# Bias rows for all 576 columns in place of rows for distances, in an attention and MLP kernel on one core

## The chip, the cores and the metric

The kernel runs on one core of a Trainium2 chip. The time is the device time of one execution in microseconds. Three runs of the kernel before gave 711.92, 712.65 and 712.97 us; their median is 712.65 us. One more execution was recorded by the hardware profiler. On a core, TensorE (PE in the profile) multiplies matrices, VectorE (DVE), ScalarE (ACT) and GpSimd (POOL) work element by element, and SyncE (SP) issues most transfers.

## What is computed

Attention with a bias made by a small network from relative positions, for 4 batches, 8 heads, 576 positions and 64 values a head, followed by a two-layer MLP over all 2304 tokens:

```python
scores = scale * np.matmul(q, k.transpose(0, 1, 3, 2))
rel = (pos[:, None] - pos[None, :]).astype(np.float32)
psi_rel = np.log1p(np.abs(rel))
psi_i = np.log1p(np.maximum(pos[:, None].astype(np.float32), 1.0))
x = (psi_rel / psi_i)[..., None]
h = np.maximum(x @ w1 + b1, 0.0)          # 32 hidden units
bias = h @ w2                             # 8 heads
scores = scores + bias.transpose(2, 0, 1)[None, :, :, :]
attn = softmax(scores); attn_out = attn @ v
...
h = x @ w_in; g = np.maximum(h, 0.0) + alpha * np.minimum(h, 0.0)
out = g @ w_out                           # 512 -> 2048 -> 512
```

The bias does not depend on the batch. For a query i and a key j it depends on |i - j| and on i, and the reference spells the softmax with its maximum taken off.

## The kernel before

The program is written as a list of some 2,800 operations, each with its choices of engine. Nothing is ordered at run time: a table `ISSUE` holds the order of all operations and the engine chosen for each (`58` is operation 58 by its first choice, `66.1` by its second), a table `SLOT` the buffer of every value, and a table `IDLE` the places where TensorE gets matmuls that compute nothing, to keep it busy (`796:2` puts two of them ahead of operation 796; they are issued by L994). Each engine works through its own part of the list in order. Numbers count the operations in the order in which the program makes them.

The stages are these. `bias_tile` (L465), 36 times, makes the bias of 16 query positions for all 8 heads, 128 rows, and writes it to a scratch in DRAM. `weights` (L645), 8 times, unpacks and splits the weights of 256 hidden columns. `qk_turn` transposes queries and keys, `v_rows` prepares values. `unit` (L752), 32 times, does the attention of two heads for 256 or 320 queries: it loads bias rows from the scratch, multiplies (L601 in float32 for batch 0, L602 in float16 pairs for the others), adds the bias and takes the maximum (L796), exponentiates (L799), normalises (L809 to L820), transposes (by TensorE at L828 for batch 0, by DMA at L815 for the others) and multiplies by the values (L857 or L849). `chunk` runs the MLP on 256 tokens at a time, first layer at L927, second at L946. The first MLP chunk needs attention of all heads of batch 0 for its queries, and the weights.

A bias tile has four rows of hidden values, each for 4 query positions times 32 units on 128 partitions (L474 to L483). A row is relu(R + psi), where R holds log1p(distance) times a scale for distances 0 to 575, once for all partitions; a row is made for as many distances as the tile needs, max(576 - 16t, 16t + 16) for tile t. It can be made by ScalarE (L478), VectorE (L475) or GpSimd (L481). One product by TensorE (L487 to L496) turns the four rows into 128 rows of bias: it walks the distances downwards up to a column `l0` and upwards behind it, so that one relative column axis serves all 16 positions, 591 columns in three pieces, each with four matmuls of 32 output partitions. ScalarE (L506) or VectorE (L507) takes the result from PSUM, and one DMA (L510) writes it to the scratch with a row pitch that shifts each position by one element, so that the loads of `unit` (L769, L782) read rows of 576 in true columns.

At the start, the constants (R, psi and its inverse, the identity and a mask; 900 columns) are loaded by L419, w1 by L416, and VectorE scales R (L426) behind a maximum over w1 (L421).

Of the kernel before, what the change touches and what calls it, by code (L numbers as in the profile page):

```python
# [25 lines left out]
RW = S  # L26
SK = 15
HQ = S + 32
IQ = H * HQ - 1
# [114 lines left out]
"""  # L144
IDLE = """
30:23 62:2 118:2 90:1 104:1 111:2 683:2 55:3 97:3 132:1 641:2 676:4 959:1 662:1 139:2 634:2 697:1 160:2 669:4 718:5 725:4 704:1 711:1 739:7 388:1
569:3 549:2 767:1 563:1 353:3 596:3 611:1 800:1 419:1 614:1 806:2 814:8 828:4 796:2
"""

# [118 lines left out]
def attention_then_moe(ctx: ExitStack, tc, q, k, v, w1, b1, w2, w_in, w_out, alpha, cst, out):  # L268
# [64 lines left out]
    def rows_of(blk, at, dims):  # L333
        x = scr[blk]
        return bass.AP(x.tensor, x.offset + 16 + at, dims)


    o_ = lambda name, val: opt.get(name, val)
    col = [0]
# [706 lines left out]
```

## Time and profile before

| | |
|---|---|
| median of three runs | 712.65 us |
| profiled execution | 711.24 us |
| its span, first to last instruction | 709.5 us |
| busy: TensorE, VectorE, ScalarE, GpSimd | 673.0, 513.7, 397.4, 167.7 us |
| matmuls that compute nothing (L994) | 111 |
| bias products (L496) | 864 records, 24 a tile |

Busy time says how long an engine had an instruction at work, not whether the end of the kernel waited for it. TensorE runs at one of two clock levels, and the profile gives the granted share of the upper one. What an engine waited for, and what ended the wait, is read from the views of waits and of the chain that ended last.

### The profile page before, as it was taken

The page shows a single profiled execution, that of the slowest core. Times are in us where ns is not written, and L with a number is a line of the kernel's source. Part 1 is how long each engine was busy: PE and PEld are TensorE (multiplying, and loading weights), DVE is VectorE, ACT ScalarE, POOL GpSimd, SP SyncE. Part 2 cuts the span into 40 slices and gives each one's busy share as a digit, 9 for nine tenths or more (in the row PEclk, how much of TensorE's full clock was granted, in tenths as well). Part 3 has the DMA queues.
Part 4 walks back from the last instruction along what each step waited for, and adds up shares of the span by engine and source line. Part 5 has one row for each costly group of instructions (what it writes and reads, how often), then busy time and mean ns, then how long its engine had stood idle before and what let it go on. Part 6 is the DMA issues. An engine that isn't in the chain of part 4 may idle for free.

```text
span 709.5 us, 15371 instructions
## 1 busy us (share of the span) xinstructions
PE 673.0 (95%) x5732; PEld 422.9 (60%) x5732; DVE 513.7 (72%) x1245; ACT 397.4 (56%) x809; POOL 167.7 (24%) x223
## 2 busy tenths in 40 slices
PE   7988878879999999999999999999999999999997
PEld 2554434445765666666666666666666666666664
DVE  6799999997898789897878777677666755333222
ACT  3888989676776566564565655644454534221321
POOL 1124253223222132221213130221221221111110
PEclk8999999999999999999999999999999999999999
DMA  9899987855589889999999998999788885100000
GB/s 208 218 296 303 289 296 255 283 183 152 117 199 219 185 175 219 222 215 190 219 198 221 194 202 161 177 211 205 170 188 190 173 142 109 19 30 1 30 1 30
DMA packets 236554, 125.89 MB, mean 177 GB/s; under 512 B 204864, under 2 KB 204864, under 8 KB 236480
## 3 DMA queue, kind: packets, MB, share of 16 engines
q1 hardware_dynamic: 233888, 124.90, 75.8%
q8 instruction: 45, 0.74, 0.5%
q10 hardware_dynamic: 2592, 0.01, 0.2%
q14 instruction: 29, 0.24, 0.1%
HBM read 73.87 MB, written 15.61 MB: 126 GB/s over the span
## 4 chain that ended last, share of the span: by engine, by line
PE 71%; DVE 18%; issue 4%; DMA 3%; ACT 2%; POOL 1%; ACTq 0%; SPq 0%; DVEq 0%; POOLq 0%
PE H L927 25%; PE O L946 24%; PE S L602 6%; PE A L849 6%; DVE five L669 3%; DVE fg L796 3%; PE A L857 2%; PE S L496 2%; PE S L828 2%; PE S L576 2%; PE S L601 1%; DMA at<-a 1%; DVE wout L387 1%; DVE mg L935 1%; DVE fg L507 1%
## 5 line engine op out<-in xcount | busy, mean ns | idle before, releaser
L927 PE MATMUL H<-x,win 128*128 128x256 f16 x1728 | 200.7, 273 | 1.3 <-DVE mg L935 1.2
L946 PE MATMUL O<-wout,mg 128*128 128x512 f16 x864 | 198.7, 379 | 1.6 <-DVE st L796 0.8
L927 PEld LDWEIGHTS <-win 128*128 128x128 f16 x1728 | 166.6, 98 | 34.0 <-issue 7.1
L799 ACT ACTIVATE fg<-fg,st 128x576 f32<-128x576 f32 x144 | 110.7, 769 | 55.4 <-DVE st L796 48.0
L946 PEld LDWEIGHTS <-mg 128*128 128x128 f16 x864 | 82.0, 98 | 95.1 <-issue 6.5
L934 ACT ACTIVATE mg<-H,sm 128x256 f32<-128x256 f32 x144 | 62.3, 469 | 135.4 <-PE H L927 121.0
L935 DVE SCALAR_TENSOR_TENSOR mg<-H,sm,mg 128x256 f32<-128x256 f32 x144 | 64.8, 478 | 101.0 <-ACT mg L934 100.7
L796 DVE CUSTOM_DVE_ANT_0 fg<-S,fg 128x576 f32<-128x576 f32 x127 | 93.8, 750 | 17.3 <-PE S L602 14.9
L812 DVE SCALAR_TENSOR_TENSOR a<-fg,st,a 128x576 f16<-128x576 f32 x108 | 90.0, 834 | 21.0 <-POOL a L809 16.1
L809 POOL TENSOR_SCALAR a<-fg,st 128x576 f16<-128x576 f32 x65 | 54.1, 834 | 177.2 <-DMA at<-a 70.1
L940 POOL TENSOR_TENSOR mg<-mg 128x512 f16<-128x512 f32 x33 | 41.2, 1247 | 157.4 <-ACT mg L938 68.1
L496 PE MATMUL S<-at,w2b 128*32 128x79 f32 (+35 forms) x684 | 50.1, 345 | 8.3 <-ACT fg L506 3.4
L602 PE MATMUL S<-qk 64*128 64x288 f16 (+1 forms) x678 | 53.3, 284 | 0.7 <-DVE qk L583 0.7
L849 PE MATMUL A<-at,five 128*64 128x256 f16 (+3 forms) x720 | 51.5, 288 | 0.0
L496 PEld LDWEIGHTS S<-at,w2b 128*32 128x32 f32 x684 | 25.3, 112 | 36.7 <-issue 9.6
L602 PEld LDWEIGHTS <-qk 64*128 64x128 f16 (+1 forms) x720 | 32.7, 96 | 23.4 <-issue 17.2
L849 PEld LDWEIGHTS <-five 128*64 128x64 f16 (+1 forms) x720 | 36.0, 109 | 14.7 <-issue 11.3
L478 ACT ACTIVATE at<-cst 128x464 f32<-128x464 f32 (+17 forms) x62 | 39.1, 658 | 8.0 <-PE S L496 4.5
L810 ACT ACTIVATE a<-fg,st 128x576 f16<-128x576 f32 x43 | 32.9, 769 | 18.6 <-DMA at<-a 11.3
L481 POOL TENSOR_SCALAR at<-cst,npsi 128x416 f32<-128x416 f32 (+15 forms) x32 | 24.9, 785 | 58.0 <-PE S L496 33.2
L994 PE MATMUL H<-sm 128*128 128x512 f16 x111 | 33.5, 412 | 0.9 <-DVE w2b L405 0.9
L819 POOL TENSOR_SCALAR fg<-fg,st 128x576 f32<-128x576 f32 x29 | 23.2, 808 | 44.6 <-DVE st L804 24.6
(148 smaller groups left out, 796.2 us busy)
## 6 DMA issues: line engine op xcount, KB each, us to landing
fg<-scr SPq DMA_DIRECT2D x64, 576.0 KB, 4.9
scr<-fg SPq DMA_DIRECT2D x36, 295.5 KB, 4.5
x<-in_moe_w_in_dram SPq DMA_DIRECT2D x10, 512.0 KB, 5.4
x<-in_moe_w_out_dram SPq DMA_DIRECT2D x10, 512.0 KB, 5.4
fg<-scr SPq DMA_DIRECT2D x32, 144.0 KB, 4.9
out_dram<-mg SPq DMA_DIRECT2D x18, 256.0 KB, 2.6
five<-in_q_dram SPq DMA_DIRECT2D x32, 128.0 KB, 4.4
five<-in_k_dram SPq DMA_DIRECT2D x32, 128.0 KB, 3.8
```

The source lines that it names most:

```text
L496: nc.tensor.matmul(ps.t[32 * gl:32 * gl + 32, c:n], lhsT=w2b, rhs=x, start=True, stop=True)
L602: return [(lambda a, dst=dst, zq=zq, zk=zk, i=i: nc.tensor.matmul(dst(a), lhsT=tr16(qt)[at, 0, pr, zq, lo:lo + n], rhs=tr16(qt)[at, 1, pr, ...
L796: V(lambda x=x, sl=sl, st=st, ls=ls: nc.vector.tensor_tensor_reduce(out=in_halves(ls[x]()), in0=halves(sl[x].t), in1=in_halves(ls[x]()), s ...
L799: A(lambda x=x, st=st, ls=ls: nc.scalar.activation(ls[x](), ls[x](), AF.Exp, bias=st.t[:, x:x + 1], scale=-1.0, accum_out=st.t[:, 2 + x:3 ...
L809: pl.op([("POOL", 775, lambda x=x, rec=rec, ls=ls, a16=a16: nc.gpsimd.tensor_scalar(a16.t[:, 0:S], ls[x](), rec(), 1.0, op0=ALU.mult, op1= ...
L812: V(lambda x=x, rec=rec, ls=ls, a16=a16: nc.vector.scalar_tensor_tensor(a16.t[:, 640:640 + S], ls[x](), rec(), a16.t[:, 0:S], op0=ALU.mult ...
L849: nc.tensor.matmul(ps.t[64 * hh:64 * hh + 64, 0:w], lhsT=v5[0:hi, zv, n, 2 * pr + hh, :], rhs=at16(at)[0:hi, 5 * za + n, 320 * hh:320 * hh ...
L927: nc.tensor.matmul(hb.t[:, f, :], lhsT=win[:, fp, zw, kb, P * f:P * f + P], rhs=x[:, zx, kb, :], start=(n == 0), stop=(n == 11))
L934: A(lambda f=f: nc.scalar.activation(gf(f), hb.t[:, f, :], AF.Copy, scale=cu[:, f:f + 1]), 470, ky, [hb, t_sig], [(g, f)])
L935: V(lambda f=f: nc.vector.scalar_tensor_tensor(gf(f), hb.t[:, f, :], cs[:, f:f + 1], gf(f), op0=ALU.mult, op1=ALU.max), 475, ky, [hb, t_si ...
L940: ("POOL", 1210, lambda: nc.gpsimd.tensor_tensor(gv(1), g.t, gv(0), op=ALU.subtract))], ky, [g, (gg, 0)], [(gg, 1)], tag="g1", cont=True)
L946: nc.tensor.matmul(ob.t[:, t, :], lhsT=gg.t[:, zg, f, P * t:P * t + P], rhs=wout[:, fp, zw, f, :], start=(first and f == 0 and (zg, zw) == ...
```

## The change

R becomes a table of 1148 columns that holds the distance for a running column offset, with the partition's own position inside the group of four taken into account. A row for group g is then R from column 572 - 4g on, 576 columns, on whichever engine. The product reads the four rows in two pieces, 512 and 64 columns, forwards. The result of 576 columns goes to a scratch of plain shape (positions, heads, columns), and the loads read two neighbouring heads as one run. The tiles of `fg` lose their 16 spare columns. The tables `ISSUE`, `SLOT` and `IDLE` are new as a whole; only the head of the first and the last is shown.

```diff
-RW = S
-SK = 15
-HQ = S + 32
-IQ = H * HQ - 1
+RC = S - 4
+RW = S + RC
...
 ISSUE = """
-3 5.1 0 203 2 8.1 1 207 11.1 17 14.1 12 15.1 6.1 16.1 7.1 204 205 9.1 206 13.1 208 10.1 209 18.1 210 215 219 33 211 19 20 21 22 24 34 23 25 29 26 58
...
 IDLE = """
-30:23 62:2 118:2 90:1 104:1 111:2 683:2 55:3 97:3 132:1 641:2 676:4 959:1 662:1 139:2 634:2 697:1 160:2 669:4 718:5 725:4 704:1 711:1 739:7 388:1
-569:3 549:2 767:1 563:1 353:3 596:3 611:1 800:1 419:1 614:1 806:2 814:8 828:4 796:2
+30:30 767:1 648:3 655:2 289:3 634:3 111:2 739:2 139:2 195:2 83:2 132:2 421:1 153:4 55:4 62:5 118:2 223:1 732:3 676:6 125:4 959:2 146:3 697:2 518:3
+669:3 521:3 538:2 552:2 529:2 662:1 577:1 753:1 611:1 771:2 782:3 793:7 625:2
...
-    fg = sb.tile([P, n_f, S + 16], F32, name="fg")
+    fg = sb.tile([P, n_f, S], F32, name="fg")
...
-    scr = [dp.tile([1, (min(256, S - i) * H + 1) * HQ], F32, name=f"scr{i}") for i in range(0, S, 256)]
+    scr = [dp.tile([min(256, S - i), H, S], F32, name=f"scr{i}") for i in range(0, S, 256)]
...
-                nc.scalar.activation(hb.t[:, 0:wd], R[:, 0:wd], AF.Relu, bias=PSI[:, g:g + 1], scale=1.0)
+                nc.scalar.activation(hb.t, R[:, lo:lo + S], AF.Relu, bias=PSI[:, g:g + 1], scale=1.0)
...
-            cuts = sorted({0, l0, 512, S + SK})
-            for c, n in zip(cuts, cuts[1:]):
+            for c, n in pieces:
                 for gl in range(4):
-                    x = hs[gl].t[:, 0:wd]
-                    if n <= l0:
-                        x = bass.AP(x.tensor, x.offset + l0 - c, [list(x.ap[0]), [-1, n - c]])
-                    else:
-                        x = x[:, c - l0:n - l0]
-                    nc.tensor.matmul(ps.t[32 * gl:32 * gl + 32, c:n], lhsT=w2b, rhs=x, start=True, stop=True)
...
+                    nc.tensor.matmul(ps.t[32 * gl:32 * gl + 32, c:n], lhsT=w2b, rhs=hs[gl].t[:, c:n], start=True, stop=True)
...
-        DMA(lambda e: e.dma_start(out=rows_of(blk, row * IQ - SK, [[HQ, P], [1, S + SK]]),
-                                  in_=ev_t()[:, 0:S + SK]), P * S * 3.4, key, [ev], [(scr_tok[16 * t // P], row)])
...
+        DMA(lambda e: e.dma_start(out=scr[blk][r0:r0 + 16].rearrange("r h j -> (r h) j"), in_=ev.t), P * S * 3.4, key, [ev], [(scr_tok[16 * t // P], r0)])
...
-                last[0] = DMA(lambda e, blk=blk, r=r, L=L: e.dma_start(out=L.t, in_=rows_of(blk, P * r * IQ + hp * HQ, [[IQ, P], [HQ, 2], [1, S]])),
+                last[0] = DMA(lambda e, blk=blk, r=r, L=L: e.dma_start(out=L.t, in_=scr[blk][P * r:P * r + P, hp:hp + 2, :]),
...
-    r = np.broadcast_to(np.log1p(u.astype(np.float32))[None, :], (P, RW))
+    rel = (u[None, :] - RC - i[:, None]).astype(np.float32)
+    r = np.log1p(np.abs(rel))
```

The new issue list begins with `3 8.1 1 269 2 11.1 5 0 14.1 17 13.1 18 12.1 6.1 16.1 7.1 19 270 271`: the load of w1 is operations 5, 8, 11 and 14, the constants are 17, the maximum over w1 is 19, and 269 to 272 are the first half of a weight tile.

## Rows read from the trace of the kernel before

**Rows 1.** The page, busy us of each engine, share of the span and instructions

```profile
PE 673.0 (95%) x5732; PEld 422.9 (60%) x5732; DVE 513.7 (72%) x1245; ACT 397.4 (56%) x809; POOL 167.7 (24%) x223
```

**Rows 2.** Busy us (instructions) by stretch, granted clock, DMA share, GB/s

```profile
31.40:159.10 127.70, 106.97 (x1075) 56.50 (x1071) 123.13 (x273) 104.19 (x181) 44.85 (x59) 1.00 0.86 271
159.10:240.00 80.90, 80.43 (x632) 51.74 (x633) 67.00 (x191) 54.76 (x116) 20.45 (x32) 1.00 0.73 170
240.00:360.00 120.00, 115.11 (x980) 76.30 (x978) 100.89 (x250) 68.62 (x144) 30.47 (x40) 1.00 1.03 206
360.00:709.50 349.50, 344.08 (x2818) 225.60 (x2815) 201.38 (x478) 151.82 (x342) 66.61 (x82) 1.00 0.64 132
```

**Rows 3.** Page's group (busy, mean ns | idle), and TensorE's timeline (start us, us)

```profile
L994 PE MATMUL H<-sm 128*128 128x512 f16 x111 | 33.5, 412 | 0.9 <-DVE w2b L405 0.9
158.12 0.60 PE L994 MATMUL H<-sm 128*128 128x512 f16 x2
```

**Rows 4.** The chain that ended last (start us, us): last long VectorE entry

```profile
151.36 1.20 DVE five L669 x2
```

**Rows 5.** Timeline of TensorE at an undisturbed bias tile

```profile
24.54 1.21 PE L496 MATMUL S<-at,w2b 128*32 128x47 f32 x24
25.68 0.86 PE L576 MATMUL O<-cst,five 128*128 128x128 f32 x5
```

**Rows 6.** Groups by line: rows and evictions of the bias

```profile
L478 ACT ACTIVATE at<-cst 128x464 f32<-128x464 f32 (+17 forms) x62 | 39.1, 658 | 8.0 <-PE S L496 4.5 <-DVE cst L427 1.9 <-PE O L496 1.3
L475 DVE TENSOR_SCALAR at<-cst 128x384 f32<-128x384 f32 (+16 forms) x35 | 14.9, 453 | 5.6 <-PE S L496 5.5
L506 ACT ACTIVATE fg<-S,cst 128x591 f32<-128x591 f32 x24 | 19.8, 835 | 4.0 <-PE S L496 4.0
L507 DVE TENSOR_SCALAR fg<-S,cst 128x591 f32<-128x591 f32 x8 | 7.1, 884 | 0.0
```

**Rows 7.** Groups by line and shape on GpSimd, rows of the bias

```profile
L481 POOL TENSOR_SCALAR at<-cst,npsi 128x416 f32<-128x416 f32 x4 | 3.6, 920 | 4.1 <-PE O L496 4.1
L481 POOL TENSOR_SCALAR fg<-cst,npsi 128x560 f32<-128x560 f32 x1 | 0.7, 736 | 0.0
L481 POOL TENSOR_SCALAR at<-cst,npsi 128x576 f32<-128x576 f32 x1 | 1.1, 1117 | 0.1
```

**Rows 8.** A score product, ten transpositions, a value product; a copy by VectorE

```profile
159.77 1.19 PE L601 MATMUL S<-qk 64*64 64x288 f32 x8
...
165.32 1.24 PE S L828 x10
172.70 2.99 PE A L857 x20
...
L839 DVE COPY at<-S 128x640 f32<-128x640 f32 x3 | 2.5, 823 | 1.1 <-PE S L828 1.1
```

**Rows 9.** Transfer, SP's and VectorE's timeline, stretch and waits at the start

```profile
cst<-in_const_dram SPq DMA_DIRECT2D x1, 450.0 KB, 3.3
4.72 0.34 SPq L419 DMA_DIRECT2D cst<-in_const_dram  x1
4.73 0.43 DVE L666 TENSOR_SCALAR win<-mg 128x512 int32<-128x512 int32 x1 [2.46 <-DMA mg<-in_moe_w_in_dram]
5.20 1.42 DVE L669 SCALAR_TENSOR_TENSOR win<-mg,win 128x512 int32<-128x512 int32 x2
10.33 0.52 DVE L426 TENSOR_SCALAR cst<-cst,sm 128x576 f32<-128x576 f32 x1
10.00:20.00 10.00, 7.63 (x77) 3.38 (x81) 6.71 (x20) 6.42 (x10) 2.38 (x3) 0.66 1.01 178
DVE at L475 <- PE S L496: 5.5, 5, 2.9
```

**Rows 10.** Waits (us, times, longest), up to 165 us and behind

```profile
PEld S L496 <- POOL at L481: 4.6, 8, 1.5
POOL a L809 <- DMA at<-a: 70.1, 23, 6.6
```

More of the change, by code (lines that the diff above doesn't have):

```diff
@@ L311, in attention_then_moe @@
     n_f = 10
-    fg = sb.tile([P, n_f, S + 16], F32, name="fg")
-    c_f2 = Slots("f2", [fg[:, 2 * i:2 * i + 2, 0:S] for i in range(n_f // 2)])
-    c_f = Slots("f", [fg[:, i, 0:S] for i in reversed(range(n_f))], [{("f2", i // 2, i % 2)} for i in reversed(range(n_f))])
+    fg = sb.tile([P, n_f, S], F32, name="fg")
+    c_f2 = Slots("f2", [fg[:, 2 * i:2 * i + 2] for i in range(n_f // 2)])
+    c_f = Slots("f", [fg[:, i] for i in reversed(range(n_f))], [{("f2", i // 2, i % 2)} for i in reversed(range(n_f))])
     for i in range(n_f // 2):
@@ L330, in attention_then_moe @@
     c_st = slots("st", 10, [P, 8])
-    scr = [dp.tile([1, (min(256, S - i) * H + 1) * HQ], F32, name=f"scr{i}") for i in range(0, S, 256)]
-    def rows_of(blk, at, dims):
-        x = scr[blk]
-        return bass.AP(x.tensor, x.offset + 16 + at, dims)
+    scr = [dp.tile([min(256, S - i), H, S], F32, name=f"scr{i}") for i in range(0, S, 256)]
     o_ = lambda name, val: opt.get(name, val)
@@ L467, in bias_tile @@
         hs, made = [], []
-        r0, l0 = S - 16 * t, 16 * t + SK
-        wd = max(r0, l0 + 1)
         for gl in range(4):
@@ L472, in bias_tile, with on_dve, on_act, on_pool @@
             hb = Buf(c_h)
-            def on_dve(g=g, hb=hb):
-                nc.vector.tensor_scalar(hb.t[:, 0:wd], R[:, 0:wd], PSI[:, g:g + 1], 0.0, op0=ALU.add, op1=ALU.max)
-            def on_act(g=g, hb=hb):
-                nc.scalar.activation(hb.t[:, 0:wd], R[:, 0:wd], AF.Relu, bias=PSI[:, g:g + 1], scale=1.0)
-            def on_pool(g=g, hb=hb):
-                nc.gpsimd.tensor_scalar(hb.t[:, 0:wd], R[:, 0:wd], 3.0e38, npsi[:, g:g + 1], op0=ALU.min, op1=ALU.max)
-            made.append(pl.op([("ACT", 286 + 0.833 * wd, on_act), ("DVE", 210 + 0.521 * wd, on_dve), ("POOL", 320 + 1.03 * wd, on_pool)], key, [t_R, t_T, t_N], [hb], tag="H", cont=True))
+            lo = RC - 4 * g
+            def on_dve(g=g, hb=hb, lo=lo):
+                nc.vector.tensor_scalar(hb.t, R[:, lo:lo + S], PSI[:, g:g + 1], 0.0, op0=ALU.add, op1=ALU.max)
+            def on_act(g=g, hb=hb, lo=lo):
+                nc.scalar.activation(hb.t, R[:, lo:lo + S], AF.Relu, bias=PSI[:, g:g + 1], scale=1.0)
+            def on_pool(g=g, hb=hb, lo=lo):
+                nc.gpsimd.tensor_scalar(hb.t, R[:, lo:lo + S], 3.0e38, npsi[:, g:g + 1], op0=ALU.min, op1=ALU.max)
+            made.append(pl.op([("ACT", 766, on_act), ("DVE", 510, on_dve), ("POOL", 900, on_pool)], key, [t_R, t_T, t_N], [hb], tag="H", cont=True))
             hs.append(hb)
@@ L487, in mm @@
         def mm():
-            cuts = sorted({0, l0, 512, S + SK})
-            for c, n in zip(cuts, cuts[1:]):
+            for c, n in pieces:
                 for gl in range(4):
-                    x = hs[gl].t[:, 0:wd]
-                    if n <= l0:
-                        x = bass.AP(x.tensor, x.offset + l0 - c, [list(x.ap[0]), [-1, n - c]])
-                    else:
-                        x = x[:, c - l0:n - l0]
-                    nc.tensor.matmul(ps.t[32 * gl:32 * gl + 32, c:n], lhsT=w2b, rhs=x, start=True, stop=True)
-        PE(mm, 1260, key, hs + [t_w2], [ps])
+                    nc.tensor.matmul(ps.t[32 * gl:32 * gl + 32, c:n], lhsT=w2b, rhs=hs[gl].t[:, c:n], start=True, stop=True)
+        PE(mm, 1130, key, hs + [t_w2], [ps])
         ev = Buf(c_f)
-        ev_t = lambda: fg[:, n_f - 1 - ev.slot]
         def shift():
@@ L504, in shift, with ev_act, ev_dve @@
             return MASK[:, m:m + 1]
-        pl.op([("ACT", 935, lambda: nc.scalar.activation(ev_t()[:, 0:S + SK], ps.t[:, 0:S + SK], AF.Identity, scale=EVI[:, t:t + 1], bias=shift())),
-               ("DVE", 935, lambda: nc.vector.tensor_scalar(ev_t()[:, 0:S + SK], ps.t[:, 0:S + SK], EVI[:, t:t + 1], shift(), op0=ALU.mult, op1=ALU.add))],
-              key, [ps, t_c, t_beta], [ev], tag="ev")
-        blk, row = divmod(16 * t, 256)
-        DMA(lambda e: e.dma_start(out=rows_of(blk, row * IQ - SK, [[HQ, P], [1, S + SK]]),
-                                  in_=ev_t()[:, 0:S + SK]), P * S * 3.4, key, [ev], [(scr_tok[16 * t // P], row)])
+        def ev_act():
+            nc.scalar.activation(ev.t, ps.t[:, 0:S], AF.Identity, scale=EVI[:, t:t + 1], bias=shift())
+        def ev_dve():
+            nc.vector.tensor_scalar(ev.t, ps.t[:, 0:S], EVI[:, t:t + 1], shift(), op0=ALU.mult, op1=ALU.add)
+        pl.op([("ACT", 830, ev_act), ("DVE", 830, ev_dve)], key, [ps, t_c, t_beta], [ev], tag="ev")
+        blk, r0 = divmod(16 * t, 256)
+        DMA(lambda e: e.dma_start(out=scr[blk][r0:r0 + 16].rearrange("r h j -> (r h) j"), in_=ev.t), P * S * 3.4, key, [ev], [(scr_tok[16 * t // P], r0)])
     order = [None]
@@ L781, in unit @@
                 for hh in range(2):
-                    last[0] = DMA(lambda e, L=L, hh=hh: e.dma_start(out=L.t[64 * hh:64 * hh + 64], in_=rows_of(2, (hp + hh) * HQ, [[IQ, 64], [1, S]])),
+                    last[0] = DMA(lambda e, L=L, hh=hh: e.dma_start(out=L.t[64 * hh:64 * hh + 64], in_=scr[2][:, hp + hh, :]),
                                   64 * S * 3.4, ky, [scr_tok[4]], [(L, ("b", hh))], keep=1 - hh, after=last[0], off="kL")
```

213 rows, old and new, of tables (ISSUE, SLOT) are left out of this document.

## Prediction, made before the change was run

> **What bounds the kernel now.** I read the whole-run page first, then the busy time by stretch, then the chain of waits, then the groups by line. The page alone misleads: it has TensorE busy for 673.0 us of 709.5 and VectorE for 72% [rows 1], which looks like a kernel bound by TensorE throughout. By stretch it falls in two. From 31.4 to 159.1 us VectorE is busy 123.13 of 127.7 us and ScalarE 104.19, while TensorE has 106.97, and part of that is idle filling: the 111 matmuls of L994 compute nothing, and the last two run from 158.12 us [rows 2, 3]. From 159.1 us to the end TensorE is busy 80.43 of 80.9, 115.11 of 120 and 344.08 of 349.5 us, so it is idle for 10.8 us in 550 [rows 2]. The chain says the same: long VectorE entries up to 151 us, then almost only matmuls [rows 4]. So the time is: the moment at which TensorE has no more gap, plus the TensorE work left at that moment. Before it, an operation costs what it costs VectorE, and ScalarE behind it. After it, only TensorE work costs anything.
>
> All 36 bias tiles stand ahead of that moment, in the issue list of either kernel. That decides how each edit is priced.
>
> **The product.** An undisturbed tile at the upper clock level starts at 24.54 us and lets the next work start at 25.68: 1.14 us for 591 columns in three pieces [rows 5]. After it is 576 columns in two pieces. By columns alone that is 1.11 us, by pieces alone 0.76; I take 1.06, near the end by columns, since the pieces that go are the short ones. So it gives 1 to 14 us over 36 tiles, 3 by the value taken. None of it counts in the sum: TensorE has 20.7 us of idle and most of its fillers in that part [rows 2, 3], and its waiting there is the cover. Were the cover gone, those 3 us would be gained.
>
> **The rows.** A tile needs four rows of max(576-16t, 16t+16) distances, on average 440; after, always 576. Over 36 tiles this is 63,360 columns against 82,944. The new table also moves them: ScalarE 72 to 76 rows, VectorE 36 to 26, GpSimd 36 to 42. At 576 columns I take 0.762 us on ScalarE (0.658 at the mean, plus 130 columns at 0.83 ns), 0.505 on VectorE (0.453, plus 130 columns at some 0.4 ns), and 0.90 on GpSimd, between 0.736 for a row of 560 and 1.117 for the one row of 576 [rows 6, 7]. The evictions go from 27 on ScalarE and 9 on VectorE to 21 and 15; they cost 0.835 and 0.885 for 591 columns, so some 0.82 and 0.87 for 576 [rows 6]. Summed durations: ScalarE 69.8 to 75.1 us, VectorE 24.3 to 26.2, GpSimd 27.7 to 37.8. That is 17 us more elementwise work, 10 of it on the engine with the most room.
>
> **Where TensorE stops waiting.** The new table reorders the whole program, so the rows alone say little; the two tables can be counted. The idle string tells where each table still expects a gap. Before, the last entry is 796:2, ahead of the transposition group that starts at 159.1 us. After, it is 625:2. I counted in each issue list what stands on VectorE ahead of that point and what is left on TensorE behind it. The last layers are untouched in both: all 72 first-layer groups and 87 second-layer operations are left, and all of batches 1 to 3. The difference on TensorE: after has one two-head score product less to do (1.12 us of the 1.19 shown, since the next work starts before its end), four transposition groups (0.60 each) and one value product (2.99), by the times of these lines [rows 8]: 6.5 us less is left. On VectorE, each price 0.06 us under its duration because its next operation starts before the last has ended: rows 36 to 26, -2.6 us; evictions 9 to 15, +4.7; weight unpacking 32 short and 64 long operations to 29 and 58, -4.9 (0.43 and 0.71 each); copies out of transpositions none to 4, +3.0 (0.823 each); evictions of queries and keys none to 3, +2.1 (not seen on VectorE; by that copy of 640 columns at 0.82); score additions 24 to 26 with their small operations, +2.7; the rest -1.1. Together +3.9 us [rows 6, 8, 9]. So at this mark after stands 2.7 us better. The mark before it (814:8 and 793:7) gives another reading: VectorE 0.9 us less, TensorE 1.0 us more left, together +0.1. I take the middle, -1.3 us, with both ends kept. ScalarE ahead of the last mark has 5.7 us more (122.7 to 128.4, of 159), GpSimd 11.0 more (50.6 to 61.6): neither fills the stretch, so I put nothing for them here and the rest into a rival.
>
> **The start.** The constants grow from 900 to 1472 columns, 450 to 736 KB. Before, their transfer was issued at 4.72 us and landed 3.3 us later; at the 178 GB/s of that stretch the other 286 KB are 1.6 us, so 9.6 us, if SP issues it no sooner [rows 9]. The scaling of that table started at 10.33 us, behind 4.9 us of unpacking and a maximum, from 4.73 us on; after, only one half of a weight tile stands ahead of it, and it is 0.2 to 0.3 us longer for 1148 columns. So the rows can begin between 0.6 us earlier and at the same time as before. But VectorE has then done 4.8 us of work instead of 7.0, since the first maximum now waits for w1 ahead of all unpacking, which is queued behind it. That is +1.6 to +2.2 us that VectorE must do later. Against it: the clock was 0.66 between 10 and 20 us, the two first tiles ran at the lower level, and VectorE waited 5.5 us in all on tiles [rows 9]. The table has 30 fillers ahead of the first product, not 23, which shortens the pause in front of it by up to 1.5 us; if the clock holds, up to 3 us come back. I take +1.5, with -1 and +2.2 as ends.
>
> **The scratch.** Bias rows are written as 128 runs of 576 values, not 591, and pairs of heads are read in one run of 4608 bytes, not two of 2304. What they feed is bound by VectorE in the first part and by TensorE in the second; I put it at nothing, with up to 3 us of gain (second rival).
>
> **Sum.** -1.3 + 1.5 = +0.2 us on the profiled execution of 711.24 us (span 709.5). That execution lies 1.4 us under the median of the runs, 712.65; the difference is carried over, so 712.9 us.
>
> **Rival one, slower: rows made on GpSimd come late.** Rows on GpSimd differ far more than the columns explain: the four of 416 columns took 0.920 us on average, one of 560 took 0.736 [rows 7]. TensorE waited for such rows eight times, 4.6 us [rows 10]. After has 42 of them, all at full width. If they take 1.1 us instead of 0.9, GpSimd has 8.4 us more, in tiles that the attention units of batch 0 need; half to all of it then reaches VectorE as waiting. That gives 717 to 721 us. It decides if the mean row on GpSimd passes 1.0 us and VectorE is idle for over 9 us between 31 and 159, where it is now idle for 4.6. A rule of the Trainium skill would make this worse: the page "SBUF — State Buffer", section "Who interferes with whom", has VectorE and GpSimd share one pair of ports, and an instruction of either kind that comes second waits out the whole of the first. By that rule each of the 42 rows may wait for a row of VectorE of 0.505 us, up to 21 us on GpSimd, which would put the time at the upper end of this rival; the trace agrees as far as the spread of [rows 7] goes, but shows no owner of a port.
>
> **Rival two, faster: the counted gain comes in full and transfers get out of the way.** The later mark alone is -2.7 us, and if the clock holds at the start its cost turns to -1: together -3.7. Between 240 and 360 us TensorE was idle for 4.9 us, with the share of DMA at 1.03 [rows 2]; shorter bias loads could return 1 to 3 us of that. That gives 706 to 709.5 us. Against it: GpSimd, not TensorE, is who mostly waits for these transfers (70.1 us) [rows 10].
>
> **Rival three: the change shows in the program and not in the time.** If ScalarE and GpSimd take the wider rows into idle time and VectorE's share stays the same, the two tables differ only by their order, and the marks by what the two readings differ: 711 to 714 us, the forecast again by another way.
>
> **Chances.** The forecast with rival three: 0.53, spread over some 710.5 to 715.5, of which 0.36 within 0.2% of 712.65 (711.2 to 714.1, about what a measurement of this kernel can tell from no change), 0.07 under and 0.10 above. Rival one 0.25, all above. Rival two 0.22, all under. So faster 0.29, same 0.36, slower 0.35. The range for 8 in 10 is 707 to 720: it takes in most of both rivals. The forecast's own range is 710.5 to 715.5.
>
> **What would show it.** Right: L496 falls to 576 records and 1.05 to 1.1 us a tile; rows at 0.76, 0.51 and 0.90 us on the three engines; the last filler between 158 and 162 us; VectorE over 95% busy from 31 to 159; from there TensorE idle for 8 to 14 us. Wrong: the last filler past 165 us (rival one, or a worse start), or before 156 us (rival two); TensorE idle for over 16 us behind the last filler, which no step here foresees, since it would come from the new order in the part that TensorE fills; or the first rows starting later than 12 us.

## The result and the profile after

The kernel after took 721.92 us in the median of four runs (720.93 to 724.52), the kernel before 712.28 us (711.36 to 712.97) beside it on the same chip. The ratio is 1.0141, with an interval of 1.0127 to 1.0156: the change makes the kernel slower by 1.4%. The forecast was 712.9 us, the range 707 to 720. The profiled execution of after took 724.52 us, with a span of 722.7.

First the busy time by stretch, with the columns of [rows 2] (span, then TensorE, its weight loads, VectorE, ScalarE, GpSimd, clock, DMA share, GB/s):

```profile
0.00:31.40 31.40, 23.84 (x156) 9.90 (x157) 17.89 (x42) 12.62 (x18) 3.34 (x8) 0.84 0.71 193
31.40:159.10 127.70, 103.71 (x860) 49.34 (x853) 122.09 (x257) 108.21 (x177) 52.69 (x66) 1.00 0.80 253
159.10:175.00 15.90, 14.03 (x102) 8.79 (x102) 13.72 (x40) 11.00 (x22) 6.40 (x10) 1.00 0.69 199
175.00:240.00 65.00, 61.78 (x448) 38.41 (x445) 53.29 (x147) 40.84 (x82) 15.32 (x23) 0.97 0.68 161
240.00:360.00 120.00, 116.27 (x1010) 77.17 (x1009) 103.95 (x258) 68.00 (x146) 34.59 (x44) 1.00 0.97 204
360.00:722.70 362.70, 354.34 (x2902) 232.15 (x2900) 213.84 (x513) 156.84 (x355) 63.11 (x81) 1.00 0.66 136
```

From 31.4 to 159.1 us VectorE is 96% busy, as before [rows 2]. But it has done only 17.89 us in the first 31.4, where before it had done 21.28, and it has not caught up at 159.1 us: TensorE still waits between 159.1 and 175. The last fillers show the mark, against 158.12 us before [rows 3]:

```profile
155.34 1.69 PE L982 MATMUL H<-sm 128*128 128x512 f16 x7
...
170.81 0.60 PE L982 MATMUL H<-sm 128*128 128x512 f16 x2
```

So the part in which VectorE sets the time ends at 171.8 us, 12.7 us later than before. The kernel is slower by just this: behind the mark TensorE needs 546.3 us to its last matmul, 0.5 more than the 545.8 before.

```profile
159.10:704.90 545.80, 539.63 (x4425) 353.64 (x4425) 369.27 (x918) 273.93 (x600) 117.54 (x153) 1.00 0.74 154
```
```profile
171.80:718.10 546.30, 535.23 (x4377) 350.06 (x4377) 373.64 (x921) 267.11 (x583) 114.94 (x152) 1.00 0.74 155
```

The first line is before, the second after. By the prediction this stretch should have been shorter by the 6.5 us of work that the new order leaves less; TensorE's busy time is 4.4 us less, but its idle time there, the stretch less the busy time, went from 6.2 to 11.1 us.

The groups that answer to [rows 6, 7] (busy us, mean ns of one):

```profile
L470 ACT ACTIVATE at<-cst 128x576 f32<-128x576 f32 x66 | 48.4, 767 | 15.9 <-PE S L482 11.9 <-DVE cst L420 3.7
L473 POOL TENSOR_SCALAR at<-cst,npsi 128x576 f32<-128x576 f32 x38 | 33.3, 881 | 69.4 <-PE S L482 49.2 <-DVE npsi L424 14.7 <-PE O L482 2.6
L467 DVE TENSOR_SCALAR at<-cst 128x576 f32<-128x576 f32 x25 | 12.5, 532 | 2.0 <-PE S L482 1.9
L467 DVE TENSOR_SCALAR fg<-cst 128x576 f32<-128x576 f32 x1 | 1.2, 1186 | 0.0
```

And the start, VectorE's and TensorE's timeline (start, length, what; in brackets the idle time ahead and what ended it), against [rows 9]:

```profile
8.98 0.82 DVE L419 TENSOR_SCALAR cst<-cst,sm 128x1148 f32<-128x1148 f32 x1
14.31 0.16 DVE L418 TENSOR_TENSOR sm<-sm 128x1 f32<-128x1 f32 x1 [4.51 <-DMA x<-in_moe_w_in_dram]
...
14.83 1.44 ACT L470 ACTIVATE at<-cst 128x576 f32<-128x576 f32 x2 [3.65 <-DVE cst L420]
...
16.19 0.29 PE L429 MATMUL A<-sm,w2b 128*32 128x1 f32 x8 [6.48 <-DVE w2b L421]
...
16.95 1.94 PE L482 MATMUL S<-at,w2b 128*32 128x512 f32 x8
...
10.00:20.00 10.00, 3.81 (x30) 1.36 (x34) 3.14 (x11) 4.72 (x7) 1.65 (x2) 0.60 0.80 216
```

The table is scaled at 8.98 us, earlier than before (10.33). Then VectorE stands still for 4.51 us ahead of L418, one small operation that takes b1. The profile names the load of a weight tile as what ended this; but the operand of the line is b1, and its four loads (L410, behind L411 for w2 in ScalarE's queue) landed late:

```profile
cst<-in_const_dram SPq DMA_DIRECT2D x1, 736.0 KB, 6.8
sm<-in_b_dram ACTq DMA_DIRECT2D x4, 0.1 KB, 5.4
...
2.65 0.92 ACTq L410 DMA_DIRECT2D sm<-in_b_dram  x2
4.85 0.81 ACTq L411 DMA_DIRECT2D w2b<-in_w_dram  x2
8.53 0.86 ACTq L410 DMA_DIRECT2D sm<-in_b_dram  x2
```

Two of the four were issued at 8.53 us behind the loads of w2, and a load of b1 took 5.4 us to land (the median of the four) with the 736 KB of constants under way (6.8 us, before 3.3). The first rows begin at 14.83 us and the first product at 16.95.

### The profile page after: what moved, and what is told of

It is laid out like the page before. It is cut to its first block, busy times and chain, and to the rows that moved or that the text cites. A ratio compares the mean times of both kernels' runs of the same rounds, so it can differ in the third digit from the quotient of the medians.

```text
span 722.7 us, 14836 instructions
## 1 busy us (share of the span) xinstructions
PE 674.0 (93%) x5457; PEld 415.8 (58%) x5457; DVE 524.8 (73%) x1251; ACT 397.5 (55%) x795; POOL 175.5 (24%) x231
## 4 chain that ended last, share of the span: by engine, by line
PE 63%; DVE 9%; DMA 3%; issue 2%; ACT 1%; POOL 0%; SPq 0%; ACTq 0%; DVEq 0%; POOLq 0%
PE H L915 23%; PE O L934 23%; PE A L837 6%; PE S L590 5%; DMA at<-a 2%; DVE fg L784 2%; PE S L564 2%; DVE five L657 1%; PE A L845 1%; DVE mg L923 1%; DVE a L800 1%; PE S L816 1%; DMA five<-in_k_dram 1%; ACT mg L922 1%; PE S L589 0%
## 5 line engine op out<-in xcount | busy, mean ns | idle before, releaser
L934 PE MATMUL O<-wout,mg 128*128 128x512 f16 x864 | 198.6, 379 | 2.3 <-DVE mg L900 1.1
L934 PEld LDWEIGHTS <-mg 128*128 128x128 f16 x864 | 82.5, 98 | 95.0 <-issue 6.9
L784 DVE CUSTOM_DVE_ANT_0 fg<-S,fg 128x576 f32<-128x576 f32 x128 | 94.4, 751 | 14.7 <-PE S L590 13.2
L797 POOL TENSOR_SCALAR a<-fg,st 128x576 f16<-128x576 f32 x71 | 58.8, 829 | 171.2 <-DMA at<-a 89.7
L928 POOL TENSOR_TENSOR mg<-mg 128x512 f16<-128x512 f32 x28 | 34.7, 1238 | 171.5 <-DVE mg L926 107.3
L470 ACT ACTIVATE at<-cst 128x576 f32<-128x576 f32 x66 | 48.4, 767 | 15.9 <-PE S L482 11.9
L482 PE MATMUL S<-at,w2b 128*32 128x512 f32 (+1 forms) x464 | 46.5, 426 | 11.2 <-DVE fg L495 4.7
L473 POOL TENSOR_SCALAR at<-cst,npsi 128x576 f32<-128x576 f32 x38 | 33.3, 881 | 69.4 <-PE S L482 49.2
L482 PEld LDWEIGHTS S<-at,w2b 128*32 128x32 f32 x464 | 17.7, 111 | 44.1 <-issue 19.3
L798 ACT ACTIVATE a<-fg,st 128x576 f16<-128x576 f32 x37 | 28.4, 771 | 19.5 <-DMA at<-a 10.1
L807 POOL TENSOR_SCALAR fg<-fg,st 128x576 f32<-128x576 f32 x33 | 26.4, 810 | 49.9 <-DVE st L792 23.2
L982 PE MATMUL H<-sm 128*128 128x512 f16 x124 | 35.8, 405 | 0.9 <-DVE sm L406 0.9
```

The lines of the kernel that those rows point to most:

```text
L470: nc.scalar.activation(hb.t, R[:, lo:lo + S], AF.Relu, bias=PSI[:, g:g + 1], scale=1.0)
L482: nc.tensor.matmul(ps.t[32 * gl:32 * gl + 32, c:n], lhsT=w2b, rhs=hs[gl].t[:, c:n], start=True, stop=True)
L784: V(lambda x=x, sl=sl, st=st, ls=ls: nc.vector.tensor_tensor_reduce(out=in_halves(ls[x]()), in0=halves(sl[x].t), in1=in_halves(ls[x]()), s ...
L797: pl.op([("POOL", 775, lambda x=x, rec=rec, ls=ls, a16=a16: nc.gpsimd.tensor_scalar(a16.t[:, 0:S], ls[x](), rec(), 1.0, op0=ALU.mult, op1= ...
L934: nc.tensor.matmul(ob.t[:, t, :], lhsT=gg.t[:, zg, f, P * t:P * t + P], rhs=wout[:, fp, zw, f, :], start=(first and f == 0 and (zg, zw) == ...
```

## The experiments

The theory at the start: three separate losses, a late start, more work on VectorE, and more gaps behind the mark. The rival was that the wide rows alone do it, by way of GpSimd.

**Code and order apart.** The change has two halves that run without each other: the new code, and the new tables `ISSUE`, `SLOT` and `IDLE`. Both lists number the operations alike.

```diff
 # the kernel after, with the tables of before
-3 8.1 1 269 2 11.1 5 0 14.1 17 13.1 18 12.1 6.1 16.1 7.1 19 270 271 9.1 20 21 15.1 272 10.1 22 277 24
+3 5.1 0 203 2 8.1 1 207 11.1 17 14.1 12 15.1 6.1 16.1 7.1 204 205 9.1 206 13.1 208 10.1 209 18.1 210
...
```

> The changed program with the three tables (issue order, buffers, idle filling) of the kernel before. Theory O (the new order costs the time, by its start and by later gaps of TensorE; rows and product hardly matter): within 3 us of before, 710 to 715 us, first product at 12 to 13 us as before, VectorE in 31.4 to 159.1 us about as busy as before. Theory W (wider rows cost it: 17 us more elementwise work on engines that are full): 718 us or more, and the last filler several us behind the 158.1 us of before.

It took 715.85 us, a ratio of 1.0049 (1.0034 to 1.0063), with a span of 713.0: between the two theories. The converse:

```diff
 # the kernel before, with the tables of after
-30:23 62:2 118:2 90:1 104:1 ...
+30:30 767:1 648:3 655:2 289:3 ...
```

> The kernel before with the three tables of the changed one. Theory O: 716 to 722 us, with VectorE idle for 4 us before the first rows as in the changed kernel. Theory W: 710 to 714 us, since the rows are as narrow as before; the start alone would cost at most some 3 us. The constants are 450 KB here and not 736, so a start that is good again in this run puts the cost of the start on their size and not on the order.

It took 716.65 us, 1.0062 (1.0042 to 1.0082), with a span of 714.3, at the lower end of theory O. By the medians the code alone costs 3.6 us, the order alone 4.4, and both together 9.6: 1.7 us appear only together, which is no more than the three intervals leave open (some 2 us). (The profiled execution of after lies 2.6 us above its median; in spans the three are 3.5, 4.8 and 13.2 us, and the tail below names 1.7 of the surplus.)

Where each sits is read from three numbers of a profile: the mark (the start of the work behind the last filler), VectorE's busy time ahead of it, and VectorE's idle time ahead of it, summed from its timeline. Busy time counts every operation that starts ahead of the mark whole; where the head of the list is that of before, one of them runs some 0.3 us past the mark, so that busy and idle time exceed the mark by as much.

| | mark | VectorE busy | VectorE idle | TensorE idle behind the mark |
|---|---|---|---|---|
| before | 159.1 | 144.7 | 14.7 | 6.2 |
| new code, old order | 163.4 | 149.1 | 14.6 | 5.7 |
| old code, new order | 165.2 | 146.9 | 18.3 | 11.0 |
| after | 171.8 | 151.1 | 20.6 | 11.1 |

The code adds busy time on VectorE and no idle time. The order adds some busy time, 3.6 us of idle time ahead of the mark, and nearly 5 us of TensorE's idle time behind it. The two add up in VectorE's busy time (144.7 + 4.4 + 2.2 = 151.3, measured 151.1).

**The start.** In after's list I put the loads of b1 (6, 9, 12, 15) ahead of the rest of w2's, and a weight tile's load (277) forward:

```diff
-3 8.1 1 269 2 11.1 5 0 14.1 17 13.1 18 12.1 6.1 16.1 7.1 19 270 271 9.1 20 21 15.1 272 10.1 22 277 24
+3 8.1 1 269 2 11.1 5 277 0 14.1 17 12.1 6.1 9.1 15.1 13.1 16.1 7.1 10.1 18 19 270 271 20 21 272 22 24
```

> The changed kernel with one edit at the head of its issue order: the second weight tile goes ahead of the constants, and the loads of b1 and w2 follow w1 at once, as in the kernel before; everything behind is unchanged. If the stall of VectorE from 9.8 to 14.3 us (waiting for b1) is on the path: the first product at 12 to 13.5 us instead of 16.95, and 3 to 5 us less than the changed kernel, about 717 to 719 us. If VectorE makes it good before TensorE is full: no difference, 721 to 723 us.

It took 718.42 us, 1.0078 (1.0053 to 1.0104) of before, 3.5 us less than after; the first bias product comes at 14.43 us, later than expected. The mark moved from 171.8 to 169.1 us.

```profile
11.55 0.82 DVE L419 TENSOR_SCALAR cst<-cst,sm 128x1148 f32<-128x1148 f32 x1 [3.16 <-DMA cst<-in_const_dram]
...
12.82 1.44 ACT L470 ACTIVATE at<-cst 128x576 f32<-128x576 f32 x2
```

b1 is there in time now, and VectorE waits 3.16 us for the constants themselves instead: behind the weight tile that I moved forward, they were issued at 6.07 us, in after at 1.75. What the loads of b1 alone would give, without that move, no run shows. The rows begin at 12.82 us, 2.0 earlier than in after and 1.5 later than before (11.28). With the old code in the new order, where the constants are 450 KB, they begin at 13.00:

```profile
12.48 0.16 DVE L425 TENSOR_TENSOR sm<-sm 128x1 f32<-128x1 f32 x1 [3.80 <-DMA sm<-in_b_dram]
...
13.00 1.44 ACT L478 ACTIVATE at<-cst 128x576 f32<-128x576 f32 x2 [2.97 <-DVE cst L427]
```

So the new order makes b1 late by itself (1.7 us at the first rows), and with the new code, whose constants are 736 KB, it is later by another 1.8 (14.83). With the new code in the old order the rows begin at 11.66 us: there the larger table costs only 0.4 us. This may be most of what the code and the order do only together: the marks move by 4.3, 6.1 and, together, 12.7, of which 2.3 are over the sum, and the early b1 takes 2.7 back.

**The wide rows, all and one engine at a time.** In the kernel before, one line makes every row 576 wide and changes nothing else:

```diff
-        wd = max(r0, l0 + 1)
+        wd = S
```

> The kernel before with every row made for 576 distances, read and written otherwise as before (same result, same order, same start). Theory W: 5 us or more above before, some 718 us, with TensorE's last filler later by as much. Theory O: within 2 us of before. By durations: VectorE's 36 rows cost 0.05 us more each (1.8 us), ScalarE's 72 0.11 (7.6 us), GpSimd's 36 0.15 (5 us); where VectorE alone bounds that part, 2 us.

It took 717.71 us, 1.0077 (1.0053 to 1.01). The mark went from 159.1 to 164.9, VectorE's busy time from 144.7 to 150.2. All of the new code in the old order has its mark at 163.4, ahead of this, so the rest of the new code may give something back; the intervals of the two ratios overlap. Then the same width for the rows of one engine only, with `wd` still the width of the others:

```diff
-nc.scalar.activation(hb.t[:, 0:wd], R[:, 0:wd], ...
+nc.scalar.activation(hb.t[:, 0:S], R[:, 0:S], ...
```

and so for GpSimd (`nc.gpsimd.tensor_scalar`) and VectorE (`nc.vector.tensor_scalar`).

> The kernel before with ScalarE's 72 rows alone made for 576 distances (8 us more on ScalarE). Theory V (only VectorE's busy time sets where TensorE stops waiting; it rises by its own rows and by what GpSimd's longer rows hold up): within 1 us of before, VectorE's busy time ahead of the last filler at 144.7 us as before, the last filler 0 to 1 us later. Theory S (ScalarE, 90% busy from 70 to 130 us, is the second bound): 3 us or more above before, with VectorE idle by as much more.

> The kernel before with GpSimd's 36 rows alone made for 576 distances (some 5 us more on GpSimd, whose own path has over 100 us of idle time). Theory V with port sharing: 1.5 to 2.5 us above before, VectorE's unpacking L666 longer by 1 to 1.5 us in sum, its idle time unchanged. If GpSimd's rows only came late (the rival of the prediction): 2 us or more, with VectorE's durations as before and its idle time up. If neither: within 0.5 us.

> The kernel before with VectorE's 36 rows alone made for 576 distances. Theory V: 1.8 to 2.5 us above before, all of it busy time of VectorE. With ScalarE's and GpSimd's parts the three runs should sum to the 5.4 us of the run with all rows wide.

| wide rows on | time, us (ratio to before, interval) | mark | VectorE busy | VectorE idle |
|---|---|---|---|---|
| none (before) | 711.83 | 159.1 | 144.7 | 14.7 |
| ScalarE, 72 rows | 714.20 (1.003, 1.0013 to 1.0048) | 160.2 | 144.7 | 15.8 |
| GpSimd, 36 rows | 713.73 (1.0027, 1.0014 to 1.0039) | 161.8 | 147.4 | 14.7 |
| VectorE, 36 rows | 714.39 (1.0035, 1.0018 to 1.0053) | 161.1 | 147.8 | 13.6 |
| all | 717.71 (1.0077, 1.0053 to 1.01) | 164.9 | 150.2 | 15.0 |

The last line was timed beside other runs of before, with a median of 712.28 us.

The three marks move by 1.1, 2.7 and 2.0 us, together 5.8, which is what all rows do at once; the three times add up less well, to 6.8 us against 5.4. Each engine costs something, and VectorE's rows are not half of it. ScalarE's act by way of a wait: its 8 us more (47.2 to 55.1 in rows) give 1.1 us of idle time on VectorE. Its run took 2.4 us more, under the 3 of theory S and over the 1 of theory V; its profile has 7.9 us of TensorE's idle time behind the mark, before 6.2. GpSimd's rows act otherwise: VectorE's idle time is the same, and its busy time grows by 2.7 us, although none of VectorE's own instructions changed. The groups of VectorE's unpacking (L666, L669) show where. Before:

```profile
L669 DVE SCALAR_TENSOR_TENSOR win<-x,win 128x512 int32<-128x512 int32 x10 | 6.9, 688 | 0.2
L666 DVE TENSOR_SCALAR five<-mg 128x512 int32<-128x512 int32 x5 | 2.1, 430 | 0.0
L666 DVE TENSOR_SCALAR wout<-mg 128x512 int32<-128x512 int32 x4 | 1.7, 417 | 0.0
```

With the wide rows on GpSimd alone:

```profile
L669 DVE SCALAR_TENSOR_TENSOR win<-x,win 128x512 int32<-128x512 int32 x10 | 7.2, 724 | 0.2
L666 DVE TENSOR_SCALAR five<-mg 128x512 int32<-128x512 int32 x5 | 2.4, 473 | 0.0
L666 DVE TENSOR_SCALAR wout<-mg 128x512 int32<-128x512 int32 x4 | 2.8, 693 | 0.1
...
L481 POOL TENSOR_SCALAR at<-cst,npsi 128x576 f32<-128x576 f32 x32 | 28.4, 896 | 56.4 <-PE S L496 25.9 <-PE O L496 13.1 <-DMA five<-in_q_dram 11.2
```

The four operations of the last group took 693 ns on average instead of 417, three of them 762 to 821 and one 418, while GpSimd's rows grew from a mean of 785 to 896. All 32 of L666 together went from 13.7 to 15.2 us. The timeline has one of the three, the first two lines from before, the other two with the wide rows on GpSimd:

```profile
69.40 0.54 POOL L481 TENSOR_SCALAR at<-cst,npsi 128x336 f32<-128x336 f32 x1
70.31 0.42 DVE L666 TENSOR_SCALAR wout<-mg 128x512 int32<-128x512 int32 x1
...
70.69 1.47 POOL L481 TENSOR_SCALAR at<-cst,npsi 128x576 f32<-128x576 f32 x2
71.67 0.77 DVE L666 TENSOR_SCALAR wout<-mg 128x512 int32<-128x512 int32 x1
```

In before GpSimd's row has ended at 69.94 us and the operation takes 0.42 us. In the other run it starts while a row of GpSimd runs, to 72.16 us, and ends 0.28 us behind that row. So do all lengthened operations of L666, six in this run and two in before: they start 0.24 to 0.45 us behind the start of a GpSimd instruction and end 0.28 us behind its end. It goes the other way too: at 100.49 us L666 starts 0.06 us ahead of a row of GpSimd and takes 0.42 us, and that row takes 0.97 us instead of some 0.74. The Trainium skill, page "SBUF — State Buffer", section "Who interferes with whom", has a pair of ports shared by VectorE and GpSimd, held for a whole instruction; these lengthened operations agree with it. No row names the owner of a port.

**The clock at the start.** The kernel before with a longer string of fillers ahead of the first product:

```diff
-30:23 62:2 118:2 ...
+30:36 62:2 118:2 ...
```

> The kernel before with 36 instead of 23 idle matmuls ahead of its first product, to hold the clock while VectorE prepares the constants. If the lower clock from 12.4 to 19.3 us is on VectorE's path (it waits 5.5 us for tiles there): 1 to 3 us under before, 709.5 to 711.5 us, the first tile 1.2 to 1.5 us long instead of 3.1. If VectorE's early waiting is made good later, or the fillers run into the product: no difference, or up to 1 us more.

It took 710.11 us, 0.998 (0.9963 to 0.9997) of before: the one version here whose interval lies below before, and narrowly. The mark does not show it: it is at 160.4 us in this profile, whose execution took 712.38 us. TensorE's pause ahead of the bias network's small product goes from 3.37 us to 0.43, and the clock holds: 1.00 from 0 to 31.4 us, where before the stretch 10 to 20 us has 0.66 [rows 9]. But the clock dips later, and the profile shows 0.92 from 100 to 130 us, before 1.00:

```profile
0.00:31.40 31.40, 28.40 (x268) 14.26 (x270) 21.71 (x57) 19.67 (x30) 5.08 (x11) 1.00 0.87 209
...
100.00:130.00 30.00, 25.32 (x210) 14.57 (x208) 27.93 (x70) 25.19 (x46) 11.25 (x15) 0.92 0.82 272
```

**Rows from VectorE to ScalarE.** If VectorE's busy time sets the mark, work taken from it should bring the mark forward. On top of the 36 fillers, 12 of its 36 rows went to ScalarE:

```diff
-... 66.1 ... 686.1 ... 110.1 ...
+... 66 ... 686 ... 110 ...
```

> The kernel before with 36 fillers ahead of the first product, and with 12 of the 36 rows of VectorE made by ScalarE. VectorE loses 12 rows of 0.45 us, 5.4 us; ScalarE gains 12 of 0.66 us, 7.9 us. Theory (the busy time of VectorE sets the last filler, at 0.65 us for each us as in the run with wide rows on VectorE, ScalarE's at 0.14 as in the run with wide rows on ScalarE): last filler 2.4 us earlier than with the 36 fillers alone, the time near 708 us. Rival: ScalarE, busy for 125 of the first 160 us, is now the one that is late; VectorE's idle time grows by what it was spared, and the time is 710 to 713 us.

It took 711.86 us, 0.9996 (0.9982 to 1.001). VectorE's rows fell from 16.3 to 10.6 us and its busy time ahead of the mark from 144.6 to 141.1, its idle time rose from 16.1 to 19.2, and the mark went from 160.4 only to 160.0. The rival's numbers came: VectorE's idle time grew by 3.1 of the 3.5 us that it was spared. ScalarE, with 25.68 of 28.6 us between 31.4 and 60 (before 23.02), is the likely one to be late in VectorE's place, by way of TensorE: VectorE's rows wait 7.1 us in all for the bias product, 3.3 with the 36 fillers alone, and that product waits 5.9 us for ScalarE's evictions and rows.

```profile
31.40:60.00 28.60, 25.65 (x310) 13.84 (x308) 25.86 (x55) 25.68 (x42) 8.47 (x15) 1.00 1.00 292
60.00:100.00 40.00, 33.62 (x387) 17.17 (x382) 36.11 (x70) 35.67 (x62) 16.58 (x18) 1.00 0.89 293
```

VectorE, 38.98 us busy of 40 between 60 and 100 us in before, has 36.11 here. ScalarE has 35.82 us there in before, so neither engine has much room, which fits that added work shows wherever it lands.

**The gaps behind the mark.** Two hybrid lists: the kernel after with its own list up to the last filler and the old order behind it, and the kernel before with its own list up to there and the new order behind it (a few buffers are renamed where lifetimes meet).

```diff
 # e9: the kernel after, behind operation 846
-625 809 847 848 623 836 626.1 870 ...
+968 969 366.1 367 970 439 440 971 ...
 # e10: the kernel before, behind operation 451
-796 620 450 621 843 797 820 830 ...
+4 796 620 797 621 624 808 843 ...
```

> The kernel before with its own list up to the last filler (the first 790 operations) and the rest in the order of the kernel after. The last filler should stay near 159.1 us. Theory: idle behind the mark rises from 6.5 to some 11 us and the time from 711.8 to some 716.5 us. Rival: the idle time stays at 6.5 us and the time within 711 to 713 us.

It took 719.17 us, 1.0095 (1.0072 to 1.0117), more than expected. The head is as in before (mark 158.8), and behind it TensorE is idle for 13.2 us instead of 6.2. Its waits behind 175 us (total, times, longest), and under them those of after:

```profile
PE O L1004 <- DVE mg L970: 2.3, 2, 1.7
PE H L985 <- DVE mg L993: 2.1, 4, 1.0
PE S L634 <- ACT at L896: 1.2, 1, 1.2
PE S L634 <- DVE qk L641: 1.2, 1, 1.2
PE S L634 <- DVE st L854: 1.1, 1, 1.1
```
```profile
PE H L915 <- DVE mg L923: 2.1, 4, 1.0
PE S L564 <- ACT at L826: 1.2, 1, 1.2
PE S L564 <- DVE qk L571: 1.2, 1, 1.2
PE O L934 <- DVE mg L900: 1.1, 2, 0.7
```

Most of them are the same waits in the two kernels, by what waits and how long: the first-layer products behind VectorE's part of the activation (2.1, four times), a transposition of queries or keys behind a copy (1.2) and behind an earlier eviction (1.2). Neither wait of 1.2 us is in the kernel before or in the new code with the old order. Some are longer here than in after (2.3 against 1.1 for L1004 and L934), which is part of the excess over the expectation; another part is 2.6 us more of TensorE's busy time than before behind the mark (542.2 against 539.6), with the granted clock at 0.50 between 334.4 and 337.7 us in this profile. So the gaps belong to the new order and come with it behind the old head too.

> The kernel after with its own list up to the last filler (the first 800 operations) and the rest in the order of the kernel before; some buffers behind the mark are renamed. The last filler should stay near 171.8 us. Theory: the new order leaves TensorE 5 us more gap behind the mark, so the idle time there falls from 11.4 to some 6.5 us and the time from 721.9 to some 717 us. Rival: the gaps come from what is late at the mark (VectorE and ScalarE enter it with less done ahead), so another order behind it has the same 11 us, and the time stays within 720 to 723 us.

It took 728.16 us, 1.0229 (1.0209 to 1.0248): neither the theory nor its rival. The seam is at fault:

```profile
176.60 1.06 ACT L720 ACTIVATE wout<-five 128x1024 f16<-128x1024 f32 x1 [7.14 <-DVE five L715]
...
178.39 1.33 PE L874 MATMUL S<-cst,fg 128*128 128x128 f32 x5 [9.24 <-ACT at L884]
```

In the old order a weight operation on ScalarE (L720) comes next, and in the new head the weights it needs are not unpacked yet. ScalarE stands 7.14 us at it, the copy L884 is queued behind, and TensorE waits 9.24 us for that copy. From there to the last matmul TensorE is idle for 6.3 us, and the longest of its waits are those of the old order:

```profile
178.40:720.90 542.50, 536.20 (x4377) 352.32 (x4377) 365.50 (x902) 268.20 (x588) 114.03 (x148) 0.99 0.74 154
...
PE S L622 <- DVE st L842: 1.3, 2, 1.0
PE H L973 <- DVE mg L981: 1.2, 2, 0.7
```

So behind the seam the old order has some 6 us of gaps here too. That it would have them without the seam is not shown, since the other engines could get ahead while TensorE stood for 9.24 us; a gain, if there is one, was lost there.

On top of it, the edit of the early b1 shown above:

> The kernel after with the old order behind the last filler, and b1 loaded ahead of the constants. Theory (start and tail are separate losses and add): 5 us less for the tail and 3.5 us less for the start, 721.9 to some 713.4 us. Rival: one of them hides the other, and the time stays above 716 us.

It took 725.56 us, 1.0184 (1.0164 to 1.0203), 2.6 us under the run without the early b1, with a seam of 9.41 us. The early start is worth 2.6 us in this list and 3.5 in that of after, so another order behind the mark does not hide it. What the tail is worth, and that 713.4 us can be reached, is not shown.

## Why the prediction was wrong

**What bounds the kernel** was read rightly. VectorE sets the time up to the last filler, TensorE behind it, and the loss sits at the mark (12.7 of 13.2 us of span). Two of the signs named for a wrong forecast came: the last filler past 165 us (170.81) and first rows later than 12 us (14.83). VectorE's 95% between 31 and 159 us came too (95.6%) and told nothing, since the loss lies on both sides of that stretch.

**The rows' own prices** came out: 0.767 us on ScalarE (0.762 said), 0.881 and 0.946 on GpSimd (0.90), 0.532 on VectorE (0.505; the mean of 25 rows, 0.513 without the longest). The product has 576 records and takes 1.11 us in an undisturbed tile, the price by columns alone (1.06 said); its gain shows nowhere, as said.

**VectorE's sum** was +3.9 us and measured +6.4 (144.7 to 151.1). By kind, each operation 0.06 us under its duration as in the prediction: unpacking −4.9 (−4.9 said), evictions +4.7 (+4.7), copies +3.0 (+3.0), queries and keys +2.1 (+2.1), rows −1.3 (−2.6), additions with their small operations and the rest +2.8 (+1.6). The mis-sized terms are the rows and the rest, 1.3 and 1.2 us. Two of VectorE's 26 rows took 0.98 and 1.19 us, the others 0.51: each of the two starts while a row of GpSimd runs. Counting all of VectorE's operations ahead of the mark that ran beside a GpSimd instruction and were over 0.08 us longer than the usual length of their line and shape, I estimate the surplus at 1.9 us before, 4.4 with the wide rows on GpSimd and 5.2 in after. The difference of 3.3 us is more than the 2.5 by which VectorE's sum missed.

**GpSimd at nothing** was a failed step. Its added time was foreseen (+11.0, measured 50.2 to 60.5), but its price was sought in room: whether it fills the stretch. It has room, and still costs, since VectorE's instructions get longer beside it: 2.7 us for 36 wide rows in the run with these alone. **ScalarE at nothing** failed too, by 1.1 us for 8 us more, as idle time of VectorE.

**The start** was the step that failed in kind. The prediction had the rows begin at the same time as before or up to 0.6 us earlier, and put +1.5 us, with +2.2 as the upper end, for unpacking that VectorE does later. I followed the scaling of the table, which came even earlier (8.98 us), but not the loads of b1, which the same list moved in ScalarE's queue behind those of w2. The first rows began at 14.83 us, 3.5 later than before, and by 31.4 us VectorE had done 3.4 us less than before (17.89 against 21.28). Of the 3.5 us, 1.7 come with the order alone and 1.8 more with the new code in it, whose constants are larger. The early b1 gets 2.7 us back at the mark.

**Behind the mark** the 6.5 us less work was right (533.5 us busy in the kernel with the early b1, against 539.6). That it makes the kernel faster by as much was not: the order also brings 5 us of new gaps. The prediction had read 10.8 us of idle time from the mark to the end of the span, foreseen 8 to 14 and put a loss from the order at over 16. By that measure, which takes in 4.6 us behind the last matmul, after has 15.6 us: outside what was foreseen, and still under the sign named for it. In after's own profile a stretch at the lower clock level behind a gap of 1.25 us costs the rest; a value product of 20 matmuls in it takes 4.75 us, before 2.99 [rows 8]:

```profile
210.00:213.40 3.40, 3.40 (x16) 1.34 (x12) 2.75 (x5) 1.03 (x3) 0.00 (x0) 0.50 0.00 0
```

**The sum** by these: mark +12.7 (VectorE's work 6.4, its idle time 5.9, and 0.4 by which its last operation lies otherwise to the mark), tail +0.5 (work −6.1, gaps +4.9, clock +1.7), 13.2 us of span. The forecast's own, by the later reading, was −2.7 + 1.5 = −1.2 us. The halving between two readings of the mark had no part in the miss: at the earlier mark after is late as well, 158.7 us against 152.8.

**The rivals.** Rival one named the right engine and the right side, 717 to 721 us, but by rows that come late and VectorE waiting for them. Neither of its conditions was met: the mean row took 0.89 us over 42 rows, not over 1.0, and VectorE is idle for 5.6 us between 31.4 and 159.1, not over 9. TensorE's weight loads, which waited 4.6 us for such rows before [rows 10], wait 2.2 us in after. The prediction put the cost of the shared ports on GpSimd's rows alone; the runs show it on VectorE's instructions as well, and there it counts. Of rival two, the clock did not hold at the start (0.60 between 10 and 20 us, before 0.66), where the pause of 3.37 us grew to 6.48; transfers gave nothing back, as TensorE's idle time between 240 and 360 us is 3.7 us against 4.9, with other waits. Rival three is refuted by the code alone, which costs 0.5%, and by the order alone with 0.6%, where 711 to 714 us were said.

What stays open: 3.6 us of VectorE's idle time belong to the order alone, of which the late b1 is a part that no run separates in the old code; which single moves in the list cause the gaps behind the mark; and whether the old order behind the mark of after would close them.

## What to carry to other kernels

Price an operation on a shared path by every engine it touches: a neighbour with room to spare can still lengthen the instructions of the engine that sets the time, and a run that widens one engine's work alone shows it in the other's mean durations. When a list is reordered, follow every operand of the first operation on the path, down to the smallest load and its place in its queue, and not only the largest transfer. And count work left behind a mark together with the gaps that the new order brings there.

## What was unexpected of the hardware

VectorE's operations on 128x512 int32, 0.42 us when alone, took 0.49 to 0.82 us where they started 0.24 to 0.45 us behind the start of a GpSimd instruction that ran on, and ended 0.28 us behind it; a row of GpSimd that started 0.06 us behind one of them took 0.97 us instead of some 0.74. Loads of 0.1 KB took 5.4 us to land with 736 KB of constants under way in the new order and 4.4 with 450 KB; in the old order they took 3.8 and 3.7. So the place in the queue counts, and the bytes showed only in the new order. A pause of TensorE of 3.37 us at the start went with the lower clock level behind it, one of 0.43 us did not; but holding the level there by fillers brought only 0.2%. The dip of that profile from 100 to 130 us (0.92) is not its price alone: the run with the wide rows on GpSimd, which has the pause, dips there too (0.91 from 120 to 140).
